# Causal block attention feeding a channel mix: seven of eight batches move from key chunks of 128 to key blocks of 64, on 64x64 and 64x32 tiles of the matrix array

## The chip, the core and the metric

The kernel runs on one core of one Trainium2 chip. The metric is the device time of one execution in microseconds. Five engines work side by side, each through its own list in order: PE (TensorE, the matrix products; its weight loads are shown as PEld), DVE (VectorE), ACT (ScalarE), POOL (GpSimd) and SP (SyncE), which here only issues DMAs. The median of three runs before is 274.98 us (273.97 to 275.21).

## The reference

```python
# q, k, v: (8 batches, 8 heads, 576 positions, 64)
scores = (1 / sqrt(64)) * q @ k.T
mask = block_i >= block_j            # blocks of 64 positions, 9 x 9 blocks
attn = softmax(where(mask, scores, -1e9))
x = (attn @ v) with heads side by side        # (8, 576, 512)
x_prev = x one position earlier in its batch (zero at the start)
xk = mu_k * x + (1 - mu_k) * x_prev
xr = mu_r * x + (1 - mu_r) * x_prev
kk = relu(xk @ w_k)                  # 512 -> 1024
out = sigmoid(xr @ w_r) * ((kk * kk) @ w_v)   # 1024 -> 512
```

The mask is causal by blocks of 64: a query sees its own block of keys and all earlier ones. Exponentials are taken without subtracting a maximum; the sum of each row is formed as a product with ones, and the sigmoid is built from a tanh.

## The kernel before, in words

**The order is written out.** The function adds some 1,380 tasks to a list (`add`), each with the engines that may do it, and `Plan.order` (L128) emits them as two tables say: `ORDER` (L17) is the order of all tasks, and in it `+n` stands for n dummy products (`unread`, L268: 128x128 products with the identity, line L273) that PE runs ahead of the task; `PLACE` (L98) gives the engine of each task that has a choice. Since every engine takes its own list in order, an instruction that has to wait holds up all that follow it on its engine.

**Rings.** Tiles come from rings of buffers (L176). In PSUM there are 8 banks of 2 KB per partition: `s` holds two tiles of two banks (scores), `m` two tiles of one bank (transposes of q and k, and attention outputs), `mm` two tiles of one bank (the channel mix). A task that takes a tile waits until the readers of its last use are done.

**Loads and transposes.** Batches 0 to 3 load q and k by 288 KB (`add_long`, L349); a cast makes them bf16 (`t_nl`); PE transposes them (`add_long_qkt`, L377, L394: 9 products of 64x64 a task) and ACT or DVE copies the result into `t_qkt`. Batches 4 to 7 (`add_qk`, L281) load by 128 KB pieces, cast, and let the DMA transpose (L325). The values (`add_v`, L421) come in five tiles a batch, 128 positions by 8 heads, and are cast to `VO`.

**Scores** (`add_scores`, L468; PE line L504, ACT line L526). A head has 64 channels, so two heads lie on the two halves of the array's rows. For a pair of heads and a chunk of 128 keys the product gives S^T, 128 keys by the queries that see them: 512, 64 + 448 and 320 + 192 columns for chunks 0 to 3 (`PIECES`), so three tiles of 2 x 512 columns a pair, each followed by one exponential of 128x1024 (`t_e`). The last 64 keys of all heads fill a tile of their own (`l`: 8 products of 64 columns, and an exponential of 64x512, `EL`, L514). In a chunk of 128 keys the upper 64 may not be seen by the first 64 queries: these corners are cleared after the exponential (`zero`, L534), four memsets a pair, on POOL or DVE.

**Attention output** (`add_av`, L563; PE line L586). Four heads (group g) lie on four strips of 32 columns (tiles of 128x32): 128 keys on the rows, and as weights ones (S: the sums) or half of the values' channels (A, B). S, A and B run over queries 0 to 511 in four chunks, 512 + 384 + 256 + 128 = 1,280 columns a strip in 16 matmuls; T does S, A and B for the last 64 queries, 960 columns in 60 matmuls. Each of the eight tasks of a batch takes one `m` bank. DVE then transposes the sums (`t1` L607, `tq` L613), takes reciprocals (L620), transposes back (`t2` L629) and multiplies (`norm` T L645, A and B L651) into `XT`. There is one buffer `tt`, so the second group's `t1` follows the first group's reciprocal.

**Channel mix.** `d` (L670, L673) and `mul` (L701, L705) form xk and xr in nine chunks of 512 positions. For a chunk, `pk` (L733, 8 tasks of 4 matmuls of 512 columns), `pr` (L772, 4 of 4), `pv` (L799, 4 of 8) run on PE; relu (L745, L747), square (L755, L757), tanh (L780) and the final product `o` (L810) follow on the other engines; a store (L818) ends it.

Of the kernel before, what the change touches and what calls it, by code (L numbers as in the profile page):

```python
# [17 lines left out]
0 3 5 13 7 4 9 6 17 69+64 43 73 70 74 15 8 19 10 71+39 75 72 11 44 76 85+11  # L18
27 97 86 16 1 98 18 109+16 87 29 20 79+7 110 23 83 99 80 88 12 89 84 113+7
111 112 25 28 114 100+11 2 90 14 30 21 115 116 81+16 101 77 33 82 102 78  # L20
127+21 169 24 26 125 131 91 35 126 92 103+9 65 22 104 117+11 181 93 128 34
130 118 51 105 132 94 133 170 171 134 121+1 36 95 119 177 135 66 129+15 122
120 96 31 106 137 182 136 124 63 107 123 149 173 172 108 152 39 139+37 52
153 138 178 150 175 32 142 47 64 143 151 154 144 179 145 57 40 174 146 155
140+53 67 176 141 157 191 48 147 148 180 195+13 159 183 156 197+4 58 196 291
198 161 207+17 68 162 289 201 211 208 160 37 212 199+5 163 158 202 41 164
184 203+19 200 61 213 165 204 209+7 185 210 290 166 205+5 981 214 292 206
193 987 38 168 42 215 49 167 982 315 216 988 53 983 319 316 217 993 293 62
220 1002 186 219 295 192 989 221 194 994 297 222 50 984 995 218 45 1003 54
223 187 999 985 294 1004 224 320 996 296 189 1000 225 317 298 997 986 321  # L30
226 1001 46 322 59 990 227 998 299 318 1009+2 230 307 229 991 228 188 247+3
231 190 232 55 251 1010 248 235 313 1005 252 300 301 233 237 1011 253 303
236 1006 254 234 238 60 409 323 255 56 327 324 239 413 328 249 241 302 415
243 256 250 240 244 304 421 242 257 325+8 992 410 419 331 274 326 329 245
1019 423 332 275 246 411 330 277 414 334 258 417 1020 416 259 1012 262 536
336 333 269 422 335 1013 263 264 265 544 337 271 276 260 412 266 418 532
1014 261 340 339 267 338 420 1007 268 537 1015 1016 270 424 305 1008 273 278
272 284 309 435 279 1017 441 341 442 436 1022 530 342 285 283 287 344 306
550 439 280 447 308 346 345 440 542 286 1025 448 1023 350 281 437 314 1018
449 1026 1028 438 311 450 1027 310 1031 1029 347 425 445 351 343 1030 443  # L40
1032 543 352 531 446 1034 349 429 1033 353 545 1037 348 355 431 444 312 367
288 1038 356 358 354 1035 426 529 368 1039 533 1040 1036 359 538 371 1046
361 360 372 282 370 1041 1021 362 373 1047 363 357 433 374 1055 1048 1024
1042 364 1051 548 375 377 1056 369 365 539 366 394 661 378 432 376 451 1052
434 1043 546 395 657 452 397 1049 382 454 453 645 549 379 1044 552 551 381
1045 383 456 649 455 1050 384 1066 385 460 457 663 388 389 386 461 458 459
1067 643 380 462 1057 392 390 651 464 463 387 391 534 1053 396 540 427 430
1058 466 1054 393 1063 398 467 1059 465 399 554 470 469 468 402 1060 401 404
562 403 400 556 428 1064 472 405 488 642 407 475 487 1061 1069 473 477 476
491 558 555 1078 406 1070 563 1068 478 557 1079 535 1071 1072 1080 492 479  # L50
471 493 1087 408 494 1073 547 483 481 480 1095 1074 1088 495 484 1097 1089
482 541 474 1096 489 485 486 1098 498 559 496 1084 1062 502 655 509 1075
1085 510 1090 1065 1076 1086 553 662 1081 1077 512 650 490 664 665 1082 1091
499 764 653 564 1083 497 644 1099 503 646 1092 560 565 501 647 504 511 1100
1107 566 656 671 567 505 659 568 508 648 514 569 1108 1104 506 561 570 516
755 515 573 500 572 571 1105 658 574 1109 652 507 1093 1106 575 517 654 1110
513 577 576 518 524 1094 578 770 519 579 1111 1101 526 758 580 527 522 583
523 582 1143 581 768 1102 585 528 1144 520 601 776 586 584 521 600 525 1137
588 587 604 774 605 1113 590 589 1138 606 607 660 591 1114 1128 608 592 1115
1122 594 1129 756 593 603 1130 595 1119 1123 673 610 1124 1116 627 1120 666  # L60
1121 1134 1117 1118 630 596 1131 628 1135 675 597 1136 1125 1112 1132 1103
598 599 602 1126 1133 667 611 609 1127 757 677 615 760 762 612 775 759 769
614 678 778 616 1154 761 617 777 680 618 679 772 622 619 682 668 779 672 613
674 1155 1145 683 681 623 620 1156 686 669 685 771 625 687 684 1146 1141 688
784 676 763 1151 624 690 629 773 689 1142 621 691 765 692 766 1152 670 1139
696 868 1148 626 693 697 631 871 1140 695 694 632 637 713 1149 875 714 635
698 640 638 1150 1187 699 633 869 636 701 1157 641 639 1188 877 704 702 703
634 1158 1178 876 717 705 879 883 718 1172 1159 707 706 1179 709 870 715 782
1173 719 872 1180 700 1169 720 873 1174 1153 1175 708 1170 767 721 722 1171
1183 1176 735 716 878 874 738 1184 1185 736 723 710 1163 737 740 1186 880  # L70
1177 790 1164 1160 791 712 742 711 741 887 1166 1165 793 1161 725 792 1162
1167 780 724 794 1168 743 795 728 1198 799 788 729 796 730 1147 731 881 888
797 800 732 1199 798 891 726 801 781 1200 727 783 889 733 789 803 1195 802
734 785 804 786 805 882 1196 884 1181 885 809 895 1189 739 1182 890 744 886
806 810 1192 745 750 1190 787 1197 807 746 897 808 811 751 826 754 814 1193
893 1201 812 749 1216 747 1194 1202 817 892 1217 1203 1207 818 748 1218 1204
820 830 901 822 819 1191 1208 1205 827 821 823 753 829 1206 752 1231 894 898
1209 1229 815 1232 831 816 832 825 1227 813 1230 902 833 896 1219 1228 834
1222 836 1220 824 899 853 1213 1221 1223 856 1210 1214 1215 828 1224 1211
854 837 835 1212 903 841 900 838 848 904 840 842 843 1242 906 851 844 905  # L80
845 908 847 839 1243 912 1239 909 849 1244 846 907 910 911 850 913 855 1225
1240 914 1241 1233 852 916 915 857 1226 917 858 863 918 1234 1236 861 922
1235 866 860 919 862 923 1275 864 921 924 920 1276 1237 940 925 865 1238 939
859 1271 927 867 943 1245 1272 926 928 929 944 1257 1246 945 946 930 1258
1260 931 1247 1259 1251 933 947 932 942 1261 1252 934 941 949 1262 935 948
1254 936 1253 1266 961 1255 938 1256 1248 1267 937 964 1263 1268 962 1249
950 1250 1264 951 954 1269 1265 955 966 1277 1270 956 969 957 963 1286 958
968 1278 953 1287 1279 952 960 1288 1273 959 967 1283 965 1274 970 971 976
1280 1284 972 1285 977 980 1289 1281 979 1282 1307 975 1290 978 1292 1308
1291 1304 1293 1309 974 1301 1294 973 1305 1319 1302 1295 1303 1320 1306  # L90
1298 1296 1297 1310 1299 1300 1315 1311 1312 1317 1316 1327 1318 1330 1328
1329 1324 1331 1332 1313 1325 1321 1326 1314 1357 1322 1333 1323 1358 1336
1334 1351 1335 1337 1338 1354 1352 1348 1353 1355 1356 1345 1349 1342 1350
1346 1339 1347 1343 1344 1359 1340 1361 1341 1360 1371 1362 1365 1372 1373
1368 1366 1367 1363 1369 1377 1370 1364 1374 1378 1379 1375 1376
"""

PLACE = (  # L98
    "PPDDPDDPDPAPDAAPPADPPDADAAADADADADAAAADADDPPDDPDPPPPDDDDPDAAPAAAAAPAAD"
    "AAAADAADADAAPDDPDDPDDPDPPDPPADPAPPPPPDPPPAAPDDDDADADAPDPPDPPPDDDDPPDDA"  # L100
    "PDAPAPPPAPADPAADAAADDDADPDPDPDPDDDDPDPPPDAAPAAAAAAPDAPDPADADAPPDPPDDPD"
    "PPDPPDPAPDAAADAAADAAAPAPPDPDPPDDDPPDPDPDPDPPDPPAAAADADDAAPPPDDADPDDDPD"
    "DPPPDDDDPPPPDDAPPAPAPDAPPPAAPPAPDDPDPDDDPDDDDPDPDDAPAPDAADDADPDPAPDADP"
    "DADPADADADAAAADDAPAPAAAPADDDDDAPAAADAAAPDAADAPADDADPDAAAAAAADADPDPAAAP"
    "AADPAPADADAPDDADDPAPDAAPADAPADADADADADADAPADADADAPAPAPAD"
)


class Plan:

    def __init__(self, rings):
        self.rings = {n: [k, []] for n, k in rings.items()}
        self.tasks = []
# [28 lines left out]
def kernel(  # L145
# [27 lines left out]
    ISQ = float(1.0 / (D ** 0.5))  # L173
    PSUM = bass.MemoryType.PSUM

    RINGS = {"ld": 8, "vl": 4, "nl": 4, "nb": 4, "tl": 1, "qkt": 2, "e": 4,  # L176
             "xt": 2, "tt": 1, "rc": 2, "rt": 2, "d": 2, "xk": 3, "xr": 2,
             "kr": 3, "k2": 1, "t": 3, "o": 4, "s": 2, "m": 2, "mm": 2,
             "vo": 2, "el": 2}
    plan = Plan(RINGS)  # L180
    pools = {}
    for n, bufs in RINGS.items():
        if n in ("vo", "el", "nb", "xt"):
            continue
# [283 lines left out]
    def add_scores(b, items):  # L468
# [19 lines left out]
        def fn(eng, me):  # L488
            qkt = tiles["qkt", b]
            for it in items:  # L490
                PS = tiles["ps", b, it] = new("s", [P, 2, 512], FP)
                if it == items[0]:
                    unread(me, PS[:, 0, 0:P])
# [419 lines left out]
```

## Time and profile before

| | before |
|---|---|
| median of 3 runs | 274.98 us |
| the profiled execution | 275.54 us, its span 273.8 us, granted clock 0.998 |
| DMA | 48.79 MB in 109,911 packets, 98,480 of them under 512 B |
| costliest ACT group | L526, 96 exponentials, 94.9 us, 1,035 ns each |
| clears L534 | DVE 65 of 112 ns, POOL 63 of 217 ns |
| matmuls of L504 / L586 / L273 | 384 / 1,728 / 401 |

A task's matmuls overlap, so the duration of one (about 380 ns for 512 columns) is not its cost: the cost is the distance from the first start of one task to the first start of the next. The busy share of PE counts the tails too and hides short waits. Idle time of an engine off the path costs nothing.

### The profile page before, as it was taken

The numbers are of one execution on the slowest core, as the hardware profiler recorded it, in microseconds if no ns is written. First come the engines' busy times: TensorE is split into PE (matmuls) and PEld (weight loads), VectorE is DVE, ScalarE is ACT, GpSimd is POOL, SyncE is SP. The second block draws the span as 40 slices with busy tenths as digits, with TensorE's granted clock in tenths as the row PEclk, the third lists the DMA queues.
The fourth block names the chain that finished last, engine by engine and source line by source line (L and its number), as shares of the span: only waits on it lengthen the run. The fifth ranks groups of instructions, "written<-read, shape, count | busy, mean of one in ns | idle before, by whom it ended". The sixth has DMA issues, their size and how long they took to land.

```text
span 273.8 us, 8635 instructions
## 1 busy us (share of the span) xinstructions
PE 266.4 (97%) x3529; PEld 138.5 (51%) x3529; DVE 212.9 (78%) x458; ACT 210.3 (77%) x314; POOL 85.7 (31%) x158
## 2 busy tenths in 40 slices
PE   7999999999999999999999999999999999999994
PEld 8877785455444544444444344444444454444442
DVE  1456887889998899888859898989889899953242
ACT  1599889999899998799899899877768852560620
POOL 5232143645251310252246124344630240300500
PEclk9999999999999999999999999999999999999999
DMA  7979999989999869999899989999112101103003
GB/s 224 262 191 348 302 307 284 245 293 233 209 232 232 192 154 202 246 177 206 191 174 233 228 198 186 237 214 254 48 40 80 42 2 77 77 0 117 38 38 116
DMA packets 109911, 48.79 MB, mean 178 GB/s; under 512 B 98480, under 2 KB 98736, under 8 KB 109872
## 3 DMA queue, kind: packets, MB, share of 16 engines
q1 hardware_dynamic: 109872, 48.25, 72.7%
q8 instruction: 27, 0.44, 0.7%
q14 instruction: 12, 0.10, 0.1%
HBM read 33.56 MB, written 9.44 MB: 157 GB/s over the span
## 4 chain that ended last, share of the span: by engine, by line
PE 81%; DVE 9%; ACT 4%; issue 1%; DMA 1%; SPq 1%; POOL 0%; POOLq 0%; ACTq 0%
PE t_mm L799 20%; PE t_mm L733 19%; PE t_m L586 12%; PE t_mm L772 10%; PE t_mm L273 10%; PE t_s L504 8%; PE t_m L394 3%; ACT t_e L526 2%; DMA t_vl<-in_v_dram 1%; DVE t_kr L747 1%; DVE t_o L810 1%; DVE t_xk L701 1%; DVE t_k L757 1%; DVE t_tt L607 1%; DVE t_xr L705 1%
## 5 line engine op out<-in xcount | busy, mean ns | idle before, releaser
L526 ACT ACTIVATE t_e<-t_s 128x1024 f16<-128x1024 f32 x96 | 94.9, 1035 | 9.1 <-PE t_s L504 8.9
L733 PE MATMUL t_mm<-t_xk,WK 128*128 128x512 f16 x288 | 67.9, 379 | 0.3 <-DVE t_kr L747 0.2
L799 PE MATMUL t_mm<-WV,t_k 128*128 128x512 f16 (+1 forms) x296 | 67.0, 374 | 0.0
L757 POOL TENSOR_TENSOR t_k<-t_kr 128x512 f16<-128x512 f32 x27 | 29.3, 1091 | 55.4 <-ACT t_kr L745 41.7
L799 PEld LDWEIGHTS <-t_k 128*128 128x128 f16 x296 | 27.5, 98 | 32.5 <-issue 2.6
L733 PEld LDWEIGHTS <-WK 128*128 128x128 f16 x288 | 26.4, 97 | 33.7 <-issue 5.9
L780 ACT ACTIVATE t_t<-t_mm 128x512 f32<-128x512 f32 x36 | 21.9, 607 | 22.2 <-PE t_mm L772 17.2
L745 ACT ACTIVATE t_kr<-t_mm 128x512 f32<-128x512 f32 x50 | 29.8, 606 | 10.3 <-PE t_mm L733 9.9
L772 PE MATMUL t_mm<-WR,t_xr 128*128 128x512 f16 x144 | 36.2, 380 | 0.3 <-DVE t_kr L747 0.2
L810 DVE SCALAR_TENSOR_TENSOR t_o<-t_t,t_mm 128x512 f32<-128x512 f32 (+1 forms) x37 | 24.7, 669 | 15.1 <-PE t_mm L799 14.4
L534 POOL MEMSET t_e<- 64x128 f16 x63 | 13.3, 217 | 73.1 <-ACT t_e L526 66.1
L504 PE MATMUL t_s<-t_qkt 64*128 64x64 bf16 (+4 forms) x384 | 33.0, 277 | 0.7 <-ACT t_e L526 0.5
L586 PE MATMUL t_m<-t_e,VO 128*32 128x64 f16 (+4 forms) x1024 | 29.2, 249 | 0.9 <-DVE t_qkt L262 0.6
L273 PE MATMUL t_mm<-identb 128*128 128x128 bf16 x390 | 28.3, 230 | 1.6 <-POOL identb masks.py:199 1.4
L273 PEld LDWEIGHTS <-identb 128*128 128x128 bf16 x401 | 25.0, 103 | 5.6 <-issue 3.2
L757 DVE TENSOR_TENSOR t_k<-t_kr 128x512 f16<-128x512 f32 x26 | 18.7, 728 | 7.8 <-ACT t_kr L745 7.7
L651 DVE TENSOR_TENSOR XT<-t_m,t_rt 128x512 f32<-128x512 f32 x32 | 21.6, 687 | 4.1 <-PE t_m L586 3.8
L586 PEld LDWEIGHTS <-VO 128*32 128x32 f16 x1152 | 17.8, 95 | 12.6 <-issue 7.2
L504 PEld LDWEIGHTS <-t_qkt 64*128 64x128 bf16 x384 | 13.7, 94 | 19.1 <-issue 14.8
L705 DVE SCALAR_TENSOR_TENSOR t_xr<-t_d,MUR,XT 128x512 f16<-128x512 f32 (+7 forms) x38 | 21.5, 575 | 0.5 <-POOL t_d L673 0.3
L705 DVE SCALAR_TENSOR_TENSOR t_xk<-t_d,MUK,XT 128x512 f16<-128x512 f32 (+7 forms) x38 | 21.2, 565 | 0.1
L772 PEld LDWEIGHTS <-t_xr 128*128 128x128 f16 x144 | 12.6, 98 | 16.6 <-issue 4.2
(60 smaller groups left out, 309.3 us busy)
## 6 DMA issues: line engine op xcount, KB each, us to landing
out_dram<-t_o SPq DMA_DIRECT2D x35, 256.0 KB, 2.5
t_vl<-in_v_dram SPq DMA_DIRECT2D x32, 256.0 KB, 4.4
t_ld<-in_q_dram SPq DMA_DIRECT2D x16, 288.0 KB, 4.7
t_ld<-in_k_dram SPq DMA_DIRECT2D x16, 288.0 KB, 5.3
t_ld<-in_q_dram SPq DMA_DIRECT2D x32, 128.0 KB, 3.4
t_ld<-in_k_dram SPq DMA_DIRECT2D x32, 128.0 KB, 3.3
t_ld<-in_moe_w_k_dram SPq DMA_DIRECT2D x8, 256.0 KB, 4.9
t_ld<-in_moe_w_v_dram SPq DMA_DIRECT2D x8, 256.0 KB, 4.6
```

What stands on the lines that cost most here:

```text
L273: nc.tensor.matmul(spare.get("at", dst), identb, identb, start=True, stop=True)
L504: nc.tensor.matmul(PS[:, h, col:col + n], qkt[rows, pr, 1, kc * P:kc * P + P], qkt[rows, pr, 0, q0:q0 + n], start=True, stop=True)
L526: nc.scalar.activation(tiles["e", b, pr][:, :, i, :], tiles["ps", b, it], AF.Exp, scale=ISQ)
L586: nc.tensor.matmul(PA[j * QC:(j + 1) * QC, col + a - lo:col + hi - lo], weight(b, (g, j), kc, kk), moving(b, (g, j), kc, a, hi), start=(kc ...
L705: nc.vector.scalar_tensor_tensor(dst, dt[:, 0, lo:lo + w], (MUK1, MUR1)[n][:, cc:cc + 1], x, ALU.mult, ALU.add)
L733: nc.tensor.matmul(ps, WK[:, cc, jc * P:(jc + 1) * P], tiles["xk", c][:, cc], start=(cc == 0), stop=(cc == CCn - 1))
L745: nc.scalar.activation(kt, ps, AF.Relu)
L757: (nc.vector if eng == "DVE" else nc.gpsimd).tensor_tensor(dst, KR, KR, ALU.mult)
L772: nc.tensor.matmul(ps, tiles["xr", c][:, cc, jt * P:(jt + 1) * P], WR[:, cc], start=(cc == 0), stop=(cc == CCn - 1))
L780: nc.scalar.activation(tiles["t", c, jt], tiles["pr", c, jt], AF.Tanh, scale=0.5)
L799: nc.tensor.matmul(ps[:, 0:w], tiles["k2", c][:, jc, jt * P:(jt + 1) * P], WV[:, jc, cols], start=(jc == 0), stop=(jc == JCn - 1))
L810: nc.vector.scalar_tensor_tensor(tiles["o", c, jt, half][:, 0:w], tiles["t", c, jt][:, cols], 1.0, tiles["pv", c, jt, half][:, 0:w], ALU.a ...
```

## The change

Batch 0 is computed as before, but in the new rings. Batches 1 to 7 are computed in key blocks of 64:

- **Scores.** Two pairs of heads at a time use four tiles of 64x64: the head within the pair by the half of the rows, the pair by the half of the columns. A block of keys goes with just the queries that see it (`BLOCKS`); the first 64 queries of block 0 go into the last unit. A group of four heads has six units of 2 x 512 columns, the last of 2 x 320, each with one exponential. The `l` tile, its exponential and the clears are gone for these batches.
- **Attention output.** All eight heads at once use eight tiles of 64x32: four heads on the strips of 32 columns, two on the halves of the rows, each half writing its own bank of a double tile. S, A and B run over queries 64 to 575, 9 key blocks, 72 matmuls; T has the first 64 queries, 24 matmuls. Four tasks a batch take the place of eight.
- **PSUM.** `s` becomes one ring of three double banks for scores, transposes and attention outputs; `m` is gone. In batch 0, S and T share a double bank, and A and B use `mm`.
- **Heads and values.** The order of heads follows the tiles; q and k of batches 1 to 3 are loaded in two DMAs of 64 partitions, and the values of a batch by head, four tiles of 64 keys x 9 blocks for two heads, two DMAs each.
- **Buffers.** `t_e`: 13 buffers of one unit, not 4 of three; `o` 3, not 4.
- **Order.** `ORDER` and `PLACE` are new throughout; 267 dummy products, not 401.

```diff
 ORDER = """
...
 PLACE = (
...
-    RINGS = {"ld": 8, "vl": 4, "nl": 4, "nb": 4, "tl": 1, "qkt": 2, "e": 4,
+    RINGS = {"ld": 8, "vl": 4, "nl": 4, "nb": 4, "tl": 1, "qkt": 2, "e": 13,
              "xt": 2, "tt": 1, "rc": 2, "rt": 2, "d": 2, "xk": 3, "xr": 2,
-             "kr": 3, "k2": 1, "t": 3, "o": 4, "s": 2, "m": 2, "mm": 2,
-             "vo": 2, "el": 2}
+             "kr": 3, "k2": 1, "t": 3, "o": 3, "s": 3, "mm": 2,
+             "vo": 2}
...
     def heads(b):
-        return [4 * g + 2 * x + y if b < LONGS else 4 * g + 2 * y + x
+        if b:
+            return [4 * y + 2 * g + x
+                    for g in range(2) for y in range(2) for x in range(2)]
+        return [4 * g + 2 * x + y
                 for g in range(2) for y in range(2) for x in range(2)]
...
+                             (d[y * D:y * D + D], src[b, 4 * y + 2 * g + x]
+                              .rearrange("(p j) d -> p (j d)", j=JT))
+                             for y in range(2)] if b else [
...
+                return [(d[u * D:u * D + D].rearrange("p (t d) -> p t d", d=D),
+                         v[b, 4 * u + sc].rearrange("(t p) d -> p t d", p=D))
+                        for u in range(2)]
...
+    BLOCKS = [
+        [(0, 0, 64, 512)],
+        [(0, 1, 64, 512)],
+        [(0, 2, 128, 448), (448, 8, 512, 64)],
+        [(0, 3, 192, 384), (384, 7, 448, 128)],
+        [(0, 4, 256, 320), (320, 6, 384, 192)],
+        [(0, 5, 320, 256), (256, 0, 0, 64)],
+    ]
+    WIDTH = [512, 512, 512, 512, 512, 320]
...
+                elif b:
+                    for col, t, q0, n in BLOCKS[it[1]]:
+                        for y in range(2):
+                            for x in range(2):
+                                rows = slice(x * D, x * D + D)
+                                kq = qkt[rows, 2 * it[0] + y]
+                                nc.tensor.matmul(
+                                    PS[y * D:y * D + D, x, col:col + n],
+                                    kq[:, 1, t * D:t * D + D],
+                                    kq[:, 0, q0:q0 + n], start=True, stop=True)
...
+            for j, z in enumerate(() if b else ZEROS[i]):
...
+    def blocks(b, PA, kind):
+        if kind == "T":
+            jobs = [(kk, 0, 64 * n) for n, kk in enumerate("SAB")]
+        else:
+            jobs = [(kind, t, None) for t in range(JT)]
+        for kk, t, col in jobs:
+            i, at, q0 = PLACE_OF[t, col is None]
+            n = S - q0 if col is None else D
+            lo = q0 - D if col is None else col
+            for c in range(GH):
+                for u in range(2):
+                    rows = slice(u * D, u * D + D)
+                    nc.tensor.matmul(
+                        PA[c * QC:(c + 1) * QC, u, lo:lo + n],
+                        weight((b, rows, c, t), kk),
+                        tiles["e", b, (c // 2, i)][rows, c % 2, at:at + n],
+                        start=t == 0, stop=col is not None or t == JT - 1)
...
+            bank = "s" if b or kind == "S" else "mm"
...
-            items = [(0, 0), (0, 1), (0, 2), None] + [
-                (pr, i) for pr in range(1, HP) for i in range(3)]
+            items = [(g, i) for g in range(2) for i in range(6)]
```

## The prediction

> **What bounds the kernel now.** I read the page first, then the chain of work that ended last, then stretches of time, then PE's timeline.
>
> ```profile
> span 273.8 us, 8635 instructions
> PE 266.4 (97%) x3529; PEld 138.5 (51%) x3529; DVE 212.9 (78%) x458; ACT 210.3 (77%) x314; POOL 85.7 (31%) x158
> ...
> DMA  7979999989999869999899989999112101103003
> ...
> PE 81%; DVE 9%; ACT 4%; issue 1%; DMA 1%; SPq 1%; POOL 0%; POOLq 0%; ACTq 0%
> ```
>
> PE is busy for 97% of the span and carries 81% of the chain; the waits put down to PE are under 5 us in all. So PE's list is the bound, and what counts is how long that list is. DMA is busy nine tenths until slice 28 (about 190 us), a possible second bound there. Three stretches, cut at the first attention-output matmul of batch 0 (19.15 us), that of batch 1 (53.31) and the last matmul's end (270.2):
>
> ```profile
> 0.00:19.10 19.10, 17.73 (x284) 15.50 (x284) 7.49 (x23) 10.39 (x14) 7.58 (x24) 1.00 0.85 224
> 19.10:53.30 34.20, 33.85 (x622) 22.91 (x619) 27.12 (x60) 30.94 (x47) 13.03 (x21) 1.00 0.99 299
> 53.30:270.20 216.90, 214.80 (x2628) 100.05 (x2626) 177.87 (x375) 168.93 (x255) 65.11 (x114) 1.00 0.69 157
> ```
>
> The columns are length; busy time (instructions) of PE, PEld, DVE, ACT, POOL; granted clock, DMA share, GB/s. In the second stretch ACT is busy for 30.9 of 34.2 us: it is the next limit there. In the third no engine but PE is over 82%.
>
> **The price of PE's work**, from its timeline (start, duration, instruction; distances between starts are the cost):
>
> ```profile
> 205.38 0.61 PE L504 MATMUL t_s<-t_qkt 64*128 64x512 bf16 x6
> 205.92 1.04 PE L772 MATMUL t_mm<-WR,t_xr 128*128 128x512 f16 x4
> 206.83 1.89 PE L799 MATMUL t_mm<-WV,t_k 128*128 128x512 f16 x8
> 208.65 0.61 PE L504 MATMUL t_s<-t_qkt 64*128 64x320 bf16 x6
> 209.19 1.90 PE L799 MATMUL t_mm<-WV,t_k 128*128 128x512 f16 x8
> 210.92 1.03 PE L772 MATMUL t_mm<-WR,t_xr 128*128 128x512 f16 x4
> ...
> 212.42 0.30 PE L586 MATMUL t_m<-t_e,ones 128*32 128x64 f16 x16
> ...
> 212.89 0.41 PE L586 MATMUL t_m<-t_e,ones 128*32 128x512 f16 x4
> ```
>
> - A column: eight matmuls of 512 take 210.92 - 209.19 = 1.73 us, 0.422 ns a column.
> - A change of tile shape: the same eight ahead of a score task take 208.65 - 206.83 = 1.82 us, so about 0.10 us.
> - Halves of rows run together: a score task has 1,024 columns on each half and takes 0.54 us = 1,024 x 0.422 + 0.10.
> - Strips of columns run together: T has 60 matmuls of 64 columns on four strips, 960 a strip, and takes 212.89 - 212.42 = 0.47 us: 0.41 for columns, and no slower than 7.8 ns a matmul.
> - A dummy product: the chain has one run of 37 in 2.17 us, 59 ns each.
>
> With these, PE's list of before comes to 34.6 us for the second stretch (42,112 columns, 39 changes of shape, 219 dummies; measured 34.2) and 210.6 us for the third (465,280 columns, 134 changes, 11 dummies; measured 216.9, so 6.3 us are waits and small costs). The sum can be trusted.
>
> **The change, part by part.** The new order, as built, shows 608 score matmuls for 384 and 1,896 of attention output for 1,728.
>
> 1. *Columns.* Scores of a batch per tile: 4 x 1,536 + 4 x 64 = 6,400 before; 2 x (5 x 512 + 320) = 5,760 after. Attention output: 2 x (3 x 1,280 + 960) = 9,600 before; 3 x 2,816 + 192 = 8,640 after. 1,600 columns less, x 0.422 ns = 0.68 us a batch, 4.7 us in seven, **if all four or eight tiles run together**. No row shows both halves and strips at once. Bounds: they do (the rows above for each alone), or only as many as already seen: eight tiles as two sets of four, +8,640 x 0.422 = 3.6 us a batch, +25.5 us; four score tiles as two pairs, +17.0 us. I take the first: no row shows tiles of one shape waiting for each other.
> 2. *Short matmuls.* At 7.8 ns each, eight tiles with 64 or 128 columns are bound by their number: per batch 3 x (0.035 + 0.008) + T (24 x 7.8 ns = 0.19 for 0.08), less 0.13 that the two T tasks lose now: +0.1, 0.8 us in seven.
> 3. *Changes of shape.* 15 attention tasks a batch become 10. Counted over the whole order with the dummies: 188 before, 153 after, 35 x 0.10 = 3.5 us. Bounds for the new shapes: nothing to twice the row.
> 4. *Dummies*: 134 fewer x 59 ns = 7.9 us, if what they waited for comes earlier; see below.
> 5. *ACT*: 7 exponentials L514 (593 ns) go, and 14 of L526 shrink from 1,024 to 640 elements (a line through 1,035 and 593 ns gives 0.70 us): 7 x 0.59 + 14 x 0.33 = 8.8 us less. *Clears*: 59 fewer on DVE (6.6 us), 53 on POOL (11.5 us). DVE takes 10 more relus (0.69 us each) in exchange, so its load hardly falls. All of it lies beside PE and counts as nothing, except ACT's in the second stretch. If that cover goes, DVE (82% of the third stretch) is late next.
> 6. *SP*: 45 more issues (24 for q and k, 21 for values) x 0.43 us. SP runs 3 to 5 us ahead of the landings, so nothing; if a load were awaited at once, 0.4 us each time. Bytes and packet sizes stay.
> 7. *Waits added.* An attention tile now needs a double bank of the ring that the scores use. With three banks, the fourth tile waits for DVE: t1, tq, reciprocal, t1 (0.71 + 0.23 + 0.26 + 0.71 = 1.9 us) where it follows S's bank, twice (t1, tq, reciprocal, t2, T's norm), 4.5 us, where it follows T's. Behind the waiting matmul stands all of PE, and ACT's and DVE's channel mix behind that. Between S and the fourth tile the new order puts T, a 1.2 us tile and 1.7 to 4.3 us of channel mix: 3.1 us or more in the first case, 5.6 in the second. Covered, with 1.1 us to spare. Bounds: nothing, to 4.5 us a batch; I take nothing, and the range takes a fifth of it.
>
> **The sum**, against the profiled execution. First stretch: 163 dummies for 171, and 1,792 columns more: 19.1 + 0.7 = 19.8. Second: PE's list is 37,888 columns, 28 changes, 104 dummies: 24.9 us. ACT has 37 instructions there: 14 exponentials at 0.94 us apart, 2 short ones, 4 casts, 7 copies, 5 weights, 3 squares, one d, about 26.4 us, more than PE; before, ACT was idle 3.3 us there, I leave it half of that: 28.0. Third: 456,512 columns and 106 changes give 203.4; with the 6.3 us of before and 0.8 for short matmuls, 210.5. Last matmul at 258.3, 270.2 - 258.3 = 11.9 us earlier; 275.54 - 11.9 = 263.6. *Loads* may add a little. In the new order the scores of batch 6 and 7 come about 15 us earlier than before, and at a DMA share near 1.0 the loads can gain only what was idle: some 5 us. They stand earlier in the new list of loads, and I find a margin of 0 to 3 us. I add 0.6 us and stay 0.6 under for the median (274.98 against 275.54): **264 us** for the median, 4% less.
>
> **The rivals.**
>
> - *Tiles do not run together.* For it: never seen here in both directions. Against: each direction alone does. Eight as two sets of four: 264 + 25 = 289 us, **slower**. It decides where more than about 11 of those 25.5 us are lost, that is, where a set overlaps less than 57% with the other.
> - *PE's pace.* 240 matmuls in 3.8 us are one every 16 ns. If eight tiles were handed over at the pace of one (in the chain 18 products of 64 columns of L394 take 0.53 us, 29 ns each), a batch would cost 7.0 us: 264 + 7 x 3.1 = 286 us, slower; it decides from about 24 ns a matmul. Against it, 7.8 ns in the row of T. The Trainium skill, "TensorE: Matmul & The Clock Gate" (section "Wait — 56ns, not 53.3ns?"), says that starts never come closer than about 25 ns; by its rule alone a batch would take 6.0 us and the kernel, as an estimate, 279. The trace differs: 60 starts in 0.47 us on four strips.
> - *The ring stalls.* One wait of about 1 us a batch at a handover, seven times, and scores that start late: 264 + 7 to 10 = 271 to 274 us. For it: fewer banks and DVE at 82%; against: the cover counted above.
> - *Loads and ACT hold.* The start keeps its length (+6 us, the dummies replaced by waits), or batches 5 to 7 wait for their loads (+4 to 5): 268 to 270 us. For it: DMA at 0.99 and ACT at 90% in the second stretch.
> - *It does not do what it says*: the built order shows the counts above, so I leave it no chance.
>
> **Chances.** Forecast (257 to 267.5) 0.58; loads and ACT 0.17; ring 0.13, of which 0.04 not under 273.6; pace 0.03; tiles 0.09. The forecast, loads and ring give the range 257 to 273; outside are tiles, pace, the ring's end and a little luck. About 0.5% is what a measurement of this kernel tells from no change: faster (under 273.6) 0.84, same 0.04, slower 0.12.
>
> **What would show it.** Tiles: S, A or B of a later batch 1.2 to 1.3 us from start to start, a score task 0.54. Shapes: 0.10 us between a 64x32 task and a full one. Start: the first attention output of batch 1 at 46 to 50 us. Ring: PE idle ahead of the fourth attention tile, released by DVE's t1 or norm. Loads: PE idle ahead of scores, released by DMA. Wrong if S takes over 1.8 us, or if waits in the third stretch exceed 15 us.

## The result, and the profile after

The changed kernel is slower: median 280.08 us (276.62 to 282.53, 20 executions) against 275.00 for the kernel before on the same chip (273.75 to 276.77, 20 executions), ratio 1.014 with a 95% interval of 1.011 to 1.017. The forecast was 264 us. A ratio is formed from a kernel's fast executions alone and a median from all of them, so where many are slow the two differ.

The page of the changed kernel (profiled execution 280.93 us), the lines that answer to those shown of before:

```profile
span 278.8 us, 9043 instructions
PE 258.6 (93%) x3787; PEld 134.3 (48%) x3787; DVE 205.3 (74%) x396; ACT 198.9 (71%) x292; POOL 79.8 (29%) x112
...
q8 instruction: 29, 0.48, 0.7%
...
PE 70%; DMA 9%; SPq 5%; DVE 5%; ACT 4%; issue 3%; POOL 2%; POOLq 0%; ACTq 0%; DVEq 0%
```

PE's busy time fell from 266.4 to 258.6 us, half of the 15.3 us that steps 1 to 4 of the prediction add up to (4.7 - 0.8 + 3.5 + 7.9), and the span still grew: PE's share of the chain falls from 81% to 70%, and DMA with SP's queue, 2% before, hold 14%. The work got a little shorter and waits more than took its place. The three stretches, cut as before at the first attention matmul of batch 0 (20.62 us), of batch 1 (53.09) and at the last matmul's end (275.8; columns as before: length, PE, PEld, DVE, ACT, POOL, clock, DMA share, GB/s):

```profile
0.00:20.60 20.60, 18.51 (x276) 15.33 (x276) 8.81 (x24) 12.30 (x15) 6.19 (x22) 1.00 0.73 197
20.60:53.10 32.50, 27.88 (x517) 18.00 (x516) 25.17 (x50) 26.19 (x37) 11.48 (x18) 0.89 1.01 246
53.10:275.80 222.70, 212.24 (x3001) 101.00 (x3000) 170.92 (x321) 160.42 (x242) 62.16 (x73) 0.98 0.75 164
```

Forecast were 19.8, 28.0 and 210.5. In the second stretch the bytes per second fell from 299 to 246 at a DMA share near 1.0 in both: the DMA engines are as busy and move a sixth less (with whole loads, in fix_qk below, they move 266 GB/s there, so the halves account for some 20 of the 53). PE's timeline (start, duration, instruction, idle time ahead and its releaser) shows the steps that held, and two losses that were not foreseen:

```profile
64.24 1.15 PE L389 MATMUL t_s<-identb,t_nl 64*128 64x64 bf16 x36 [2.18 <-POOL t_nl L249]
65.33 3.51 PE L880 MATMUL t_mm<-WV,t_k 128*128 128x512 f16 x8
68.67 0.59 PE L853 MATMUL t_mm<-WR,t_xr 128*128 128x512 f16 x2
...
119.84 1.50 PE L616 MATMUL t_s<-t_e,VO 64*32 64x64 f16 x77
122.67 0.26 PE L616 MATMUL t_s<-t_e,VO 64*32 64x128 f16 x11 [1.33 <-issue]
122.87 1.04 PE L814 MATMUL t_mm<-t_xk,WK 128*128 128x512 f16 x4
...
125.56 1.39 PE L616 MATMUL t_s<-t_e,VO 64*32 64x512 f16 x72
126.89 1.04 PE L853 MATMUL t_mm<-WR,t_xr 128*128 128x512 f16 x4
127.85 0.63 PE L524 MATMUL t_s<-t_qkt 64*64 64x512 bf16 x8
128.41 1.90 PE L880 MATMUL t_mm<-WV,t_k 128*128 128x512 f16 x8
130.24 0.63 PE L524 MATMUL t_s<-t_qkt 64*64 64x448 bf16 x16
```

B (72 matmuls on eight tiles) takes 126.89 - 125.56 = 1.33 us with its change of shape, a score task 128.41 - 127.85 = 0.56, a task of 8 full matmuls ahead of a change of shape 130.24 - 128.41 = 1.83: steps 1 to 3 as forecast. But A of batch 3 stops for 1.33 us at 122.67, eleven matmuls before its end, and the profile names nothing that it waits for ("issue"). The same happens in A of batches 4 and 5.

The chain in the second stretch (start, duration, what) shows the other kind of wait:

```profile
26.71 0.47 SPq L232
...
27.22 4.76 DMA t_ld<-in_q_dram
...
32.08 0.67 ACT t_nl L243
...
33.34 1.17 PE t_s L260 x18
```

A load of q for batch 1 is issued at 26.7 us and lands 4.8 us later; cast, copy and PE wait for it. From 60 to 99 us PE stands still three more times behind loads, 2.6, 1.5 and 2.3 us from start to start: for q and for values of batch 2, and at 98 us for ScalarE, which was itself held at a late load of k for batch 4 (one of the loads that stand behind the halves in SP's list). The two longest of these waits are paid twice, as the first lines of the timeline above show: after the one at 64 us the next task of 8 full matmuls takes 68.67 - 65.33 = 3.34 us for 1.73 to 1.83, and as windows the granted clock there is 0.50, and 0.52 after the wait at 98 us:

```profile
65.30:68.60 3.30, 3.30 (x11) 1.19 (x9) 2.16 (x5) 3.23 (x6) 0.85 (x2) 0.50 0.77 225
99.70:102.90 3.20, 3.20 (x11) 1.17 (x9) 1.61 (x3) 3.17 (x6) 0.80 (x2) 0.52 1.11 246
```

These two tasks lose 1.6 and 1.5 us. No attention tile of batches 1 to 7 waits for DVE's `t1` or norm. The ring of three banks holds PE up once, early: at 24.8 us dummies, which run into the tile of the score task behind them, wait 1.0 us for DVE's norm of batch 0.

### The profile page after: what moved, and what is told of

The parts are those of the page before. It is cut to its first block, busy times and chain, and to the rows that moved or that the text cites. A ratio compares the mean times of both kernels' runs of the same rounds, so it can differ in the third digit from the quotient of the medians.

```text
span 278.8 us, 9043 instructions
## 1 busy us (share of the span) xinstructions
PE 258.6 (93%) x3787; PEld 134.3 (48%) x3787; DVE 205.3 (74%) x396; ACT 198.9 (71%) x292; POOL 79.8 (29%) x112
## 4 chain that ended last, share of the span: by engine, by line
PE 70%; DMA 9%; SPq 5%; DVE 5%; ACT 4%; issue 3%; POOL 2%; POOLq 0%; ACTq 0%; DVEq 0%
PE t_mm L814 19%; PE t_mm L880 17%; PE t_mm L853 9%; PE t_s L616 9%; PE t_s L524 6%; DMA t_ld<-in_q_dram 6%; SPq L232 5%; PE t_mm L260 4%; PE t_s L389 2%; PE t_s L260 2%; ACT t_e L555 2%; DMA t_tl<-in_k_dram 2%; POOL t_k L838 1%; DMA t_vl<-in_v_dram 1%; ACT t_qkt L243 1%
## 5 line engine op out<-in xcount | busy, mean ns | idle before, releaser
L555 ACT ACTIVATE t_e<-t_s 128x1024 f16<-128x1024 f32 (+1 forms) x96 | 89.1, 980 | 11.1 <-PE t_s L524 8.5
L861 ACT ACTIVATE t_t<-t_mm 128x512 f32<-128x512 f32 x36 | 21.4, 594 | 30.7 <-PE t_mm L853 29.4
L828 DVE TENSOR_SCALAR t_kr<-t_mm 128x512 f32<-128x512 f32 x32 | 21.7, 685 | 8.0 <-PE t_mm L814 7.5
L616 PE MATMUL t_s<-t_e,VO 64*32 64x64 f16 (+7 forms) x1120 | 21.9, 284 | 4.9 <-issue 3.7
L524 PE MATMUL t_s<-t_qkt 64*64 64x512 bf16 (+7 forms) x560 | 25.8, 293 | 0.6 <-ACT t_e L555 0.6
L786 DVE SCALAR_TENSOR_TENSOR t_xr<-t_d,MUR,XT 128x384 f16<-128x384 f32 (+7 forms) x42 | 24.1, 584 | 0.2
L616 PEld LDWEIGHTS <-VO 64*32 64x32 f16 x1120 | 16.0, 92 | 11.9 <-issue 7.5
L786 DVE SCALAR_TENSOR_TENSOR t_xk<-t_d,MUK,XT 128x192 f16<-128x192 f32 (+7 forms) x42 | 21.2, 523 | 0.0
L731 DVE TENSOR_TENSOR XT<-t_s,t_rt 128x512 f32<-128x512 f32 x28 | 18.5, 681 | 3.1 <-PE t_s L616 3.0
L754 POOL TENSOR_TENSOR t_d<-XT 128x576 f32<-128x576 f32 x10 | 11.9, 1191 | 30.3 <-DVE XT L731 11.9
L524 PEld LDWEIGHTS <-t_qkt 64*64 64x64 bf16 x560 | 11.1, 106 | 17.3 <-issue 15.2
```

The lines of the kernel that those rows point to most:

```text
L524: nc.tensor.matmul(PS[y * D:y * D + D, x, col:col + n], kq[:, 1, t * D:t * D + D], kq[:, 0, q0:q0 + n], start=True, stop=True)
L555: nc.scalar.activation(tiles["e", b, it][:, :, 0:w], tiles["ps", b, it][:, :, 0:w], AF.Exp, scale=ISQ)
L616: nc.tensor.matmul(PA[c * QC:(c + 1) * QC, u, lo:lo + n], weight((b, rows, c, t), kk), tiles["e", b, (c // 2, i)][rows, c % 2, at:at + n], ...
L786: nc.vector.scalar_tensor_tensor(dst, dt[:, 0, lo:lo + w], (MUK1, MUR1)[n][:, cc:cc + 1], x, ALU.mult, ALU.add)
L828: nc.vector.tensor_scalar_max(kt, ps, 0.0)
```

## The experiments

Theories on the loads: **P**, a DMA that fills 64 of the 128 partitions runs slower; **I**, the added issues on SP cost the time; **O**, the new order makes waits that have nothing to do with the halves. First the loads were halved in the kernel *before*, where nothing else changes, once by partitions and once by columns.

**b_half_rows**: the kernel before, q and k of batches 1 to 3 in two DMAs of 64 partitions.

```diff
                          lambda d, src=src, x=x: [
+                             (d[y * D:y * D + D], src[b, 4 * g + 2 * x + y]
+                              .rearrange("(p j) d -> p (j d)", j=JT))
+                             for y in range(2)] if b else [
                              (d, src[b, 4 * g + 2 * x:4 * g + 2 * x + 2]
```

> The kernel before, with each 288 KB load of q and k for batches 1 to 3 made by two DMAs of 64 partitions, as the changed kernel makes them; same data, same order. Theory I (each issue costs: 24 more issues at 0.5 to 0.6 us hold up the queue of loads between 17 and 65 us): slower by 4 to 10 us, 279 to 285 us, waits of PE on the loads of q and k. Theory P (a DMA into half of the partitions is itself slow): the same here. Rival O (the new order of the loads is late, the halves cost nothing): within 1 us of 275.

**b_half_cols**: the same loads in two DMAs of 128 partitions, 1,280 and 1,024 bytes each.

```diff
+                             (d[:, z * 320:z * 256 + 320],
+                              src[b, 4 * g + 2 * x:4 * g + 2 * x + 2]
+                              .rearrange("y (p j) d -> (y p) (j d)", j=JT)
+                              [:, z * 320:z * 256 + 320])
+                             for z in range(2)] if b else [
```

> The kernel before, with the same loads made by two DMAs of all 128 partitions and 1,280 and 1,024 bytes a partition: as many issues as in the run with halves of partitions, but full width. Theory I (issues): as slow as the halves of partitions, 279 to 285 us. Theory P (half the partitions): within 2 us of 275. Rival O: within 1 us of 275.

Measured, against a before of 274.91 us: b_half_rows 283.26 us, ratio 1.029 (1.024 to 1.033); b_half_cols 276.49, ratio 1.007 (1.004 to 1.010). So twenty-four more issues cost 1.6 us at most, and that each fills half of the partitions costs 6.8 more. The DMA view from 20 to 40 us (packets, MB, GB/s; then queue q1's packets, MB, share of 16 engines), kernel before:

```profile
DMA packets 4753, 6.46 MB, mean 323 GB/s; under 512 B 1981, under 2 KB 1981, under 8 KB 4749
...
q1 hardware_dynamic: 4749, 6.40, 97.1%
```

b_half_rows:

```profile
DMA packets 3138, 4.61 MB, mean 231 GB/s; under 512 B 1110, under 2 KB 1110, under 8 KB 3135
...
q1 hardware_dynamic: 3135, 4.56, 96.4%
```

b_half_cols:

```profile
DMA packets 5186, 5.75 MB, mean 287 GB/s; under 512 B 1499, under 2 KB 3847, under 8 KB 5183
...
q1 hardware_dynamic: 5183, 5.70, 92.1%
```

The share is 96 to 97% in the first two, so the engines are equally busy, yet move 6.40 and 4.56 MB. So a packet must take longer, and in the trace it does: the median packet of 2,304 bytes takes 93 ns in the kernel before and 162 ns in b_half_rows. In b_half_cols packets of 1,280 bytes take 55 ns, as 93 x 1,280 / 2,304 = 52 would have it. The slowness is not confined to the halves: the weights' packets of 2,048 bytes, whose DMAs fill 128 partitions in both runs, go from 84 to 125 ns beside them. In the changed kernel the median packet of q and k takes 130 ns in the same window. Theory P holds; why the packets slow down, no run shows.

Theory I is a fifth of it at most, and even that fifth has another claimant. Among dummies in b_half_cols PE stops for 2.1 us, waiting for nothing that the profile shows:

```profile
29.13 2.24 PE L273 MATMUL t_mm<-identb 128*128 128x128 bf16 x37
33.44 1.05 PE L273 MATMUL t_mm<-identb 128*128 128x128 bf16 x16 [2.07 <-issue]
```

The same instruction is idle for 0.25 us ahead in the kernel before and for 1.89 us in b_half_rows. The stop, whose kind is the subject of "The gaps" below, is 1.8 us longer than in the kernel before, more than the 1.6 us; so what an issue costs stays open.

**a_qk_whole** and **a_qkv_whole**: the changed kernel with one DMA of 128 partitions for each load again. The first loads two neighbouring heads of q and k of batches 1 to 3 where heads four apart are wanted, so heads are mixed up; the second mixes up the values of batches 1 to 7 too.

```diff
-                             (d[y * D:y * D + D], src[b, 4 * y + 2 * g + x]
-                              .rearrange("(p j) d -> p (j d)", j=JT))
-                             for y in range(2)] if b else [
```

> The changed kernel with q and k of batches 1 to 3 loaded by one DMA of 128 partitions each, from two neighbouring heads; for these batches heads are then mixed up, so part of the output is another one than the reference's. 24 issues fewer, same bytes. Theories I and P (the halves hold the loads up): first attention output of batch 1 at 48 to 50 us for 53.1, waits on q and k loads up to 104 us gone, 266 to 271 us. Rival O (order, or too little buffer): 278 to 281 us.

> As the run with whole loads of q and k, and the values of batches 1 to 7 too by one DMA of 128 partitions each (256-byte pieces as before, other places, so the values are mixed up as well). 52 issues fewer in all. Theories I and P: 264 to 269 us, what is left over the forecast of 264 being three gaps of 1.2 to 1.8 us inside attention output of batches 3, 4 and 5. Rival O: 278 to 281 us.

Measured: 271.07 us, ratio to before 0.979 (0.974 to 0.984), and 272.27, ratio 0.990 (0.987 to 0.994). Whole loads of q and k give 9.0 us back against the 280.08 of the changed kernel; whole loads of values add nothing (their packets have 256 bytes, and the median one takes 18 ns either way). First attention matmul of batch 1 at 50.53 us (53.09), last matmul's end at 266.8 (275.8). Theory O falls for the larger part: the same order with whole loads beats the kernel before. The three gaps inside A stayed in both.

**The gaps.** Counted from 0 in order of start, with the weight loads and the dozen synchronising instructions of PE's list, the instructions after the gaps have the numbers 3777, 4545 and 5313 in the changed kernel and in both runs with whole loads: 768 = 3 x 256 apart. And the page counts 29 pieces, 0.48 MB, on queue q8, "instruction": 16 KB each. One of them starts at 119.9, 145.1 and 171.4 us, just ahead of each gap, and takes 1.2 to 1.4 us. That gave theory **F**: PE's instructions come in blocks of 256; where a whole block lies in a burst of short matmuls it is used up before the next one is there. S, T and A are 168 matmuls, 336 instructions, in about 2.8 us; a full `pk` task is 8 instructions in 0.86. The rival **T**: the gaps belong to these tasks, through some wait that the profile does not show. Dummy products separate the two: taking some out ahead moves every later instruction within its block and changes nothing in batches 3 to 5.

For these runs the loads were cured without mixing heads. **fix_qk**: a load takes two neighbouring heads, and the pairs of a score task are chosen anew, so that everything computed is the reference's; in the written order, the first score task of batch 2 stands behind one `pv` task. **fix_qk_m28**, **fix_qk_m68**: 28 and 68 dummies fewer ahead of the first task. **fix_qk_nod**: without the 101 dummies from the end of batch 0 to batch 1's third score task.

```diff
+                deps += [t for pr in ((1 - it[0], 3 - it[0])
+                                      if 0 < b < LONGS else
+                                      (2 * it[0], 2 * it[0] + 1) if b else
...
-                                kq = qkt[rows, 2 * it[0] + y]
+                                kq = qkt[rows, 2 * y + 1 - it[0] if b < LONGS
+                                         else 2 * it[0] + y]
...
+                        tiles["e", b, (1 - c % 2, i)][rows, c // 2, at:at + n]
+                        if b < LONGS else
                         tiles["e", b, (c // 2, i)][rows, c % 2, at:at + n],
...
-0 3 7 5 9 4 13 8 11 6 17 69+79 10 15
+0 3 7 5 9 4 13 8 11 6 17 69+51 10 15      (fix_qk_m28; 69+11 in fix_qk_m68)
```

> The changed kernel with q and k of batches 1 to 3 again in one DMA of 128 partitions each, and its computation kept: a load holds two heads that follow each other, the pairs of a score task are chosen anew (one of each half), attention finds its exponentials accordingly, and the first score task of batch 2 stands one product later. Theory P (half the partitions cost the loads their pace): as the run with heads mixed, 271 us (270 to 273), ratio to before 0.98 to 0.99, first attention product of batch 1 at 50 to 51 us. Theory O (the new order's waits, not the loads): 278 to 281. Theory F (PE waits for its instructions where a block of 256 lies wholly in a burst of short products): gaps of 1.2 to 1.8 us inside attention of batches 3, 4 and 5, at PE instructions 3777, 4545 and 5313 counted with the weight loads, as in the three runs before it.

> The kernel fix_qk with 28 dummy products fewer ahead of the first task (51 for 79), where PE waits for the first load anyway; each is two instructions with its weight load, so every later one stands 56 earlier in its block of 256. Theory F: the gaps leave batches 3 and 4 and come at four other places, near 82, 161, 188 and 219 us, in attention of batches 2, 5, 6 and 7, 3.9 to 5.5 us in all; the time is that of fix_qk to 1.5 us more. The rival (theory T: the gaps belong to these tasks, a wait that the profile doesn't show): gaps as in fix_qk, in batches 3, 4 and 5, same time.

> The kernel fix_qk with 68 dummy products fewer ahead of the first task (11 for 79): every later instruction stands 136 earlier. Theory F: one gap is left, near 53 us in attention of batch 1, of 1.0 to 1.5 us, none in batches 3 to 7; 2 to 3.5 us less than fix_qk, 267 to 269 us. Theory T: gaps in batches 3, 4 and 5, the time of fix_qk. If the dummies at the start keep the clock up, the first stretch is longer in both.

> The kernel fix_qk without the 101 dummy products that stand between the first attention products of batch 0 and the third score task of batch 1. What the prediction's step 4 supposed (dummies stand where a product waits, so that they cost nothing as long as what it waits for comes late): the stretch from 20 to 50 us keeps its length within 1 us, with waits in their place, since loads and ScalarE set it; if PE is what sets it, it loses up to 101 x 59 ns = 6.0 us. Theory F: every later instruction stands 202 earlier, so two gaps at most are left (near 54 and 112 us, 1.3 to 2.1 us in all), and 1.5 to 3 us go from the third stretch. Theory T: gaps in batches 3, 4 and 5 as in fix_qk.

Measured (before on this chip 277.26 us, 274.61 to 277.82):

| | median us | ratio to before, 95% | first attention of batch 0, of batch 1, last matmul's end | gaps with no cause shown, over 0.5 us: instruction number (us from start to start) |
|---|---|---|---|---|
| fix_qk | 272.06 | 0.983 (0.977 to 0.989) | 19.66, 50.41, 267.36 | 961 (0.56), 3777 (1.19), 4545 (1.46), 5313 (2.00) |
| fix_qk_m28 | 270.63 | 0.978 (0.972 to 0.983) | 18.45, 49.94, 264.93 | 705 (1.06), 1985 (0.52), 2753 (0.60), 4545 (0.62), 5313 (1.45), 6081 (0.94) |
| fix_qk_m68 | 271.90 | 0.984 (0.976 to 0.992) | 20.00, 53.27, 265.95 | 961 (1.83) |
| fix_qk_nod | 268.77 | 0.969 (0.962 to 0.976) | 19.55, 49.93, 262.47 | none |

Every number leaves 193 when divided by 256, in all runs, and what stands there changes: attention of batch 0 and A of batches 3, 4, 5 in fix_qk; A of batch 0, attention of batches 1, 2, 5 and 6 and a `pk` in fix_qk_m28. The kernel before has one such place, 0.47 us among dummies. Theory T falls. A of batch 3 in fix_qk:

```profile
109.93 1.48 PE L616 MATMUL t_s<-t_e,ones 64*32 64x512 f16 x80
...
113.71 0.26 PE L616 MATMUL t_s<-t_e,VO 64*32 64x128 f16 x11 [0.97 <-issue]
113.91 1.04 PE L816 MATMUL t_mm<-t_xk,WK 128*128 128x512 f16 x4
```

In fix_qk_m68 the same tasks run through, and a stop has come into attention of batch 0:

```profile
30.99 0.33 PE L597 MATMUL t_mm<-t_e,VO 128*32 128x256 f16 x5 [1.56 <-issue]
...
111.45 1.48 PE L616 MATMUL t_s<-t_e,ones 64*32 64x512 f16 x80
112.76 1.57 PE L616 MATMUL t_s<-t_e,VO 64*32 64x64 f16 x88
114.27 1.04 PE L816 MATMUL t_mm<-t_xk,WK 128*128 128x512 f16 x4
```

S, T and A take 113.91 - 109.93 = 3.98 us in the first and 114.27 - 111.45 = 2.82 in the second. The places were forecast only in part: of four expected in fix_qk_m28 three came (batch 7's did not), and those in batches 0 and 1 and at a `pk` were not among them; one expected in batch 1 of fix_qk_m68 did not come. The times missed too: fix_qk_m28 was to be as long as fix_qk or longer and is 1.4 us shorter, since its start is; fix_qk_m68 was to be 2 to 3.5 us shorter. From batch 1 to the end, fix_qk takes 267.36 - 50.41 = 217.0 us, fix_qk_m68 212.7, fix_qk_nod 212.5: the blocks cost 4.3 to 4.4 us there. In fix_qk_m68 the start gave 2.9 us back, 1.6 of them in the new gap, so its median hardly moved.

What the places have in common is in the traces: at every stop of over 0.5 us at such a number, in all runs, PE goes on 1.2 to 1.6 us after a 16 KB piece on q8 has landed (in A of batch 3 of the changed kernel at 122.67, the piece at 121.15). So theory F needs a supplement: it is not the short block alone that counts, but how late its successor comes. In fix_best below, the 256 instructions ahead of number 3521 are used up in 2.1 us too, yet their piece had begun 0.8 us before PE entered them, and 0.1 us is lost. In b_half_cols the piece began only 3.9 us after, and PE stopped although the block had lasted 4.1 us.

**after_nod**: the changed kernel, loads in halves, without the 101 dummies. **fix_best**: fix_qk without 28 of the dummies ahead of the first task and 73 of the 101, which leaves 18 and 10 at two waits of batch 1. **b_half_2q**: b_half_rows with the second half issued by ScalarE.

```diff
-69+79 ... 91+7 ... 193+6 ... 138+17 ... 209+5 ... 212+25 ... 215+23
+69+51 ... 91 ... 193 ... 138 ... 209 ... 212+10 ... 215      (fix_best)
...
-            for dst, src in jobs(tiles[dst_key]):
-                nc.sync.dma_start(dst, src)
+            for n, (dst, src) in enumerate(jobs(tiles[dst_key])):
+                (nc.scalar if n and two else nc.sync).dma_start(dst, src)
```

> The changed kernel itself, its loads in halves, without the 101 dummy products between the first attention products of batch 0 and the third score task of batch 1; every later PE instruction stands 202 earlier in its block of 256. If theory F (instruction blocks) and theory P (half the partitions) are two separate costs that add: the three gaps in attention of batches 3 to 5 go (4.4 us) and the waits for loads of batches 1 to 3 stay, so 275.5 to 277 us, ratio to before 1.00 to 1.008, between the changed kernel (1.014) and the run with both cured (0.969). If the two are one cost (the gaps follow from late loads): gaps stay and the time stays at 279 to 281.

> The kernel fix_qk with 101 dummy products fewer, so that PE's instructions stand in their blocks as in fix_qk_nod, but 28 of them are taken from the 79 ahead of the first task and 73 from the start of batch 1. In fix_qk_m28 the first task came at 6.4 us for 7.6 to 7.8 in the runs with all 79. If the dummies held it up there: first attention product of batch 0 at 18.3 to 18.6 us, and about 1.2 us less than fix_qk_nod, ratio to before 0.963 to 0.967. If batch 1's loads set the end of that stretch: first attention product of batch 1 at 49.9 as in fix_qk_nod, and its ratio, 0.969. No gap in attention of batches 3 to 7 in either case (theory F).

> The kernel before with q and k of batches 1 to 3 as two DMAs of 64 partitions, as in b_half_rows (283.3 us, ratio 1.0286, 231 GB/s from 20 to 40 us), but the second half issued from ScalarE's queue, so that both halves can be under way at once. If a half is slow because it reaches only half of the partitions at a time: the two together regain most of the pace, 290 to 320 GB/s, and all but 1 to 3 us of the 8.4 come back, less what ScalarE's issues cost it (24 issues). If a half is slow in itself (its transfers are as long but half as many): 230 to 250 GB/s, and the time stays at 282 us or above.

Measured, against a before of 275.46 us:

- *after_nod*: median 278.32 (273.92 to 281.29, 10 executions), ratio 1.000 (0.995 to 1.005) from four of them. The ratio falls where the sum of two separate costs was expected (1.000 to 1.008), the median 1.3 us above. The gaps of batches 3 to 5 are gone (one is left, 1.38 us, number 1729). But in the profiled execution, with 279.36 us a longer one than the four, the stretch from batch 1 to the end takes 274.3 - 51.5 = 222.8 us, no less than the 222.7 of the changed kernel: waits for loads came in their place, as these lines of DVE's and then of PE's timeline show:

```profile
209.48 0.46 DVE L249 CAST VO<-t_vl 128x576 f16<-128x576 f32 x1 [2.44 <-DMA t_vl<-in_v_dram]
209.85 0.68 DVE L891 SCALAR_TENSOR_TENSOR t_o<-t_t,t_mm 128x512 f32<-128x512 f32 x1
```

```profile
98.19 0.90 PE L389 MATMUL t_s<-identb,t_nl 64*128 64x64 bf16 x27 [4.14 <-ACT t_qkt L243]
...
210.59 2.75 PE L880 MATMUL t_mm<-WV,t_k 128*128 128x512 f16 x12 [1.31 <-DVE t_o L891]
```

  DVE waits 2.4 us for values of batch 7, and a `pv` task on PE 1.3 us for what stands behind that cast on DVE. At 98 us a transpose of batch 3 waits 4.1 us for ScalarE, which a load of q for batch 4 had held for 3.9. By the ratio, 1.014 to 1.000, the two costs add; by this one trace PE freed of one meets the other. Which of the two is usual was not settled.
- *fix_best*: 268.39 us (263.49 to 270.59, 6 executions), 0.974 by the medians, without an interval, so neither of the two ratios expected (0.963 to 0.967, and 0.969) was met. First attention matmul of batch 0 at 18.70 and of batch 1 at 46.69, 3.2 us ahead of fix_qk_nod; then PE waits 1.6 us for a load of q of batch 2, and at batch 2's S the lead is 0.4 us (79.53 against 79.89). What the start gains, the loads take back. Two stops of the kind above are left, in attention of batch 0 (1.02 and 1.19 us, numbers 705 and 961), and none in batches 3 to 7, as expected. It and fix_qk_nod are the fastest versions, 7.1 and 8.5 us under the kernel before on the same chips.
- *b_half_2q*: 295.04 us, ratio 1.071 (1.063 to 1.078). From 20 to 40 us 247 GB/s, and the median packet 128 ns, between 93 and 162. Two halves at once regain a little pace at most. The time is no clean answer: ScalarE's list now waits at 24 issues too, and how much that costs was not separated.

The second stretch of fix_qk_nod and fix_best, as windows (columns as above), shows the granted clock with fewer dummies. fix_qk_nod:

```profile
19.50:49.90 30.40, 23.71 (x413) 12.88 (x410) 24.43 (x50) 25.64 (x37) 11.98 (x19) 0.78 0.98 269
```

fix_best:

```profile
18.70:46.70 28.00, 21.95 (x443) 12.57 (x441) 24.96 (x50) 25.43 (x37) 11.39 (x18) 1.00 1.00 288
```

With twenty-eight dummies at two waits the granted clock is 1.00, with none 0.78; but with all 101 (fix_qk) it is 0.94. There is more between the two (fewer dummies at the start), so neither the clock nor the 2.4 us can be put down to the 28 dummies alone. What a low clock costs is seen in the first two `pk` tasks: in fix_qk they take 1.83 us, in fix_qk_nod 3.24, at a granted clock of 0.96 and 0.56 (39 to 43 us).

## Why the prediction was wrong, step by step

The end of the last matmul was forecast at 258.3 us and came at 275.8, 17.5 us later. The profiled executions divide this into 8.4 for the halved loads (275.8 to 267.4, fix_qk), 4.9 for what leaves with the 101 dummies (to 262.5, fix_qk_nod: 4.4 of it behind the start, where the gaps were), and 4.2 that stay: 2.4 in the second stretch (30.4 against 28.0), 2.0 in the third, 0.2 less in the first. What the last 2.0 us are was not separated.

- **Step 6 failed**: "SP runs 3 to 5 us ahead of the landings, so nothing... Bytes and packet sizes stay." They did stay, and the conclusion was wrong: a packet of the same size takes 162 ns for 93 in b_half_rows, where only the halves are new, and 130 in the changed kernel, 93 again in fix_qk. The term put at nothing measured 8.4 us: 1.0 ahead of batch 0's attention, 1.7 in the second stretch and 5.8 in the third, where PE waits for loads. From 20 to 100 us the DMA share was 0.79 to 1.00; the prediction knew of that and used it only for the loads of later batches. The values' halves, 21 of the 45 issues, cost nothing that could be measured. The Trainium skill, "DMA: Bandwidth & Descriptors" (section "Rules for kernel authors"), says that two transfers to disjoint halves of the partitions serialize, on one queue or on two, and to use one of 128 partitions. The advice agrees with the runs, 231 against 323 GB/s; the packets' pace they show beside it, and that the halves serialize no run shows by itself. This row speaks against the change, and I had not weighed it.
- **Not on the list at all**: PE's own instructions. The change turns a batch's attention output into 240 matmuls, 72 of them in 1.2 us; the prediction asked whether PE can start them that fast (it can), not whether its instructions reach it that fast. The three gaps are 4.5 us long, from start to start. The Trainium skill, "Runtime: NRT & Kernel Launch" (section "Instruction fetch mechanics"), has blocks of 16 KiB, 256 instructions, fetched ahead, the cost "mostly hidden". The block size agrees with the traces; that it is hidden holds for the kernel before (0.25 us lost in one place), and not for the three blocks here, used up in 2.0 to 2.3 us.
- Steps 1 to 3 were **right**: S 1.22 to 1.23 us from start to start, 1.32 with the change of shape, scores 0.56 and 0.48, T 0.10 to 0.22, and 0.10 for a change of shape. In the first stretch's sum, though, 1,792 columns (0.76 us) less eight dummies (0.47) give 0.3 us, not 0.7; measured 1.5.
- Step 4 (dummies, "if what they waited for comes earlier") was **half right**. It did not come earlier, so the second stretch took 32.5 us, not 28.0; with whole loads and without 101 dummies still 30.4. That is the rival "loads and ACT hold", which came true for the start, beside the failed step. Leaving dummies out is not free for the tasks behind: without the 101 the granted clock falls to 0.78 and the first two `pk` tasks take 1.4 us longer together. The stretch as a whole kept its length, 30.4 us against 30.7 with them (fix_qk).
- Step 5 was **right** as far as seen: in the third stretch PE was idle for 1.1 us behind ACT's exponential and DVE's `o` and relu, beside the waits that go back to loads. Step 7 was **right** for batches 1 to 7: no stall at the ring; one of 1.0 us came in batch 0.
- The rivals: tiles, PE's pace and the ring were the ways to "slower", and none of them happened. The kernel became slower by two mechanisms that were in no rival; 0.12 was too little for a change of this size.
- The sign given for being wrong, over 15 us of waits in the third stretch, points to the right place: load waits of 6.4 us, the two tasks at half the clock 3.1 and the gaps 4.5 come to 14.0, so by its letter the sign was not met.

## What to carry to other kernels

A load that keeps its bytes and its packet sizes can still become slower by being split over the partitions: look at how many partitions each DMA fills, above all where the DMA share is already near 1.0, and change which tile holds what rather than the load. When many short matmuls follow each other, count PE's instructions as well as columns, and when a wait "on nothing" appears, number the instructions: if the numbers repeat modulo 256, look when the piece on the instruction queue landed, and shift the instructions. Read the granted clock behind each wait of PE, and before dummies are taken out.

## What the runs showed of the hardware

- A packet of 2,304 bytes took 93 ns (median, 20 to 40 us) in DMAs that fill 128 partitions, 162 ns in DMAs that fill 64 in turn on one queue, 128 ns with the halves on two queues. Packets of 2,048 bytes in whole DMAs beside the halves on one queue took 125 ns for 84.
- PE stopped for up to 2.3 us at instructions 256 x n + 193 (counted from 0, with weight loads and synchronising instructions), and went on 1.2 to 1.6 us after a 16 KB piece on the instruction queue had landed; in the changed kernel a piece took 0.9 to 1.4 us. The 256 before had been used up in 2.0 to 2.4 us at the stops in bursts of 64x32 matmuls of batches 2 to 6, and in 3.3 to 6.9 us at the others, where the piece began 1.8 to 5.1 us after PE had entered the block. Other blocks used up in 2.0 to 2.4 us lost 0.2 us or less where the piece had landed within 1.2 us of PE's entering them.
- Eight tiles of 64x32 run together: 72 matmuls, 2,816 columns on each tile, in 1.22 to 1.23 us, 17 ns a matmul and 0.43 ns a column.
- After a wait of 2.2 us PE's next eight matmuls of 512 columns took 3.34 us for 1.73 to 1.83, at a granted clock of 0.50: a wait cost up to 1.6 us more than its own length.
